# A linear-attention and gated-MLP kernel: the first batch loaded in two halves of heads through casting DMAs, and block 0's output phase moved behind its own gate and value products

## The chip, the cores and the metric

The kernel runs on one core of one Trainium2 chip. The metric is the device time of one execution in microseconds (us). Differences under about 0.5% are not told apart from no change.

## The reference

```
kv  = einsum('bhsd,bhse->bhde', k, v)            # q, k, v: (8, 8, 576, 64) fp32
o   = einsum('bhsd,bhde->bhse', q, kv)
x   = o / sqrt(mean(o*o, -1) + 1e-6) * g_norm    # then (4608, 512): 4608 tokens, 512 = 8 heads x 64
hid = gelu(x @ w_gate) * (x @ w_val)             # (512, 1536) each
out = x + sigmoid(x @ w_res) * (hid @ w_out)     # (512, 512) and (1536, 512)
```

## The kernel before

Each batch b has 576 tokens. The first 512 of them make block b: four groups j of 128 tokens. The last 64 tokens of two neighbouring batches make one group of the ninth block (blk = 8). Everything is cast to fp16 and multiplied on TensorE (PE) into PSUM.

**Attention of a batch.** `by_token_q` and `by_token_k` (L101, L107) regroup q and k from "by head" to "by token" with a copy; `a_qT` transposes q on PE; `a_kv` (L150) sums k^T v over tokens, six pieces of 96 rows per pair of heads, and a VectorE (DVE) multiply with `mask` keeps the two diagonal 64x64 blocks; `a_o` multiplies q by it, with a square on ScalarE (ACT) and a sum on DVE; `a_norm` (L209) makes 1/rms with twelve small DVE operations; `a_t` scales; `a_xT` (L254) transposes x for the MLP; `a_x` multiplies x by g for the residual. In odd batches `a_rem_qT` and `a_rem_o` do the same for the 64 remaining tokens of two batches.

**MLP of a block.** `m_gval` (L291) makes one slice f of 128 hidden features: 4 matmuls of 512 columns with w_gate, 4 with w_val, a gelu on ACT and a product on DVE into `hid`. There are 12 slices. `m_out(blk, j)` (L312) makes the output of 128 tokens: 4 matmuls with w_res, 12 with w_out, then tanh, two DVE operations and a store.

**Order.** Each engine runs its instructions in the order in which the program issues them. The loop at L431 goes over nine blocks. A block has 12 slots of `m_gval`, then four of `m_out` of the block before it; the last block has four more for its own. `attn_plan(blk + 1)` (L407) spreads the next batch's attention over the slots, one list of steps per slot. In block 0 there is no block before, so there are 12 slots only, and the plan starts in slot 7: its later steps stand behind the last slot, with no MLP work between them. The loads of later batches are issued from GpSimd's queue (POOL), which casts fp32 to fp16 on the way; `load_batch` needs the `kr` and `qraw` buffers free.

**Start.** Batch 0 is loaded in fp32 from SyncE's queue (SP), q, then k and v in halves of heads (L346 to L350), cast and regrouped by ACT, DVE and POOL (L381 to L391), multiplied, normalised in four groups of 512 columns (`a_norm_by_sqrt`, L230) and then transposed group by group inside `m_gval_first` (L300), which runs slices f = 0 and 1 for one group of tokens (a chunk) at a time. The weights' loads are issued behind the cast of v on POOL (L388).

Of the kernel before, what the change touches and what calls it, by code (L numbers as in the profile page):

```python
# [18 lines left out]
def kernel(  # L19
# [15 lines left out]

# [51 lines left out]
    def tiles_16(b):  # L87
        b16_t[b, "q"] = qkvp.tile([P, NJ, H, D], FP16, tag="q16", name="q16")
        b16_t[b, "k"] = qkvp.tile([KP, NI, H, D], FP16, tag="k16", name="k16")
        b16_t[b, "v"] = qkvp.tile([KP, H, NI * D], FP16, tag="v16", name="v16")  # L90

    def load_batch(b):
        tiles_16(b)
        raw[b, "k"] = stage.tile([KP, H, NI * D], FP16, tag="kr", name="kr")
        raw[b, "q"] = stage.tile([P, H, NJ * D], FP16, tag="qraw", name="qraw")
        nc.gpsimd.dma_start(out=raw[b, "k"], in_=src_kv(k, b, 0, H))  # L96
        nc.gpsimd.dma_start(out=b16_t[b, "v"], in_=src_kv(v, b, 0, H))
        nc.gpsimd.dma_start(out=raw[b, "q"], in_=src_q(b, 0, H))
        load_qr(b)

    def by_token_q(b, lo, hi, copy):  # L101
        copy(
            out=b16_t[b, "q"].rearrange("p j h d -> p h j d")[:, lo:hi, :, :],
            in_=raw[b, "q"].rearrange("p h (j d) -> p h j d", j=NJ)[:, lo:hi, :, :],
        )

    def by_token_k(b, lo, hi, copy):  # L107
        copy(  # L108
            out=b16_t[b, "k"].rearrange("p i h d -> p h i d")[:, lo:hi, :, :],
            in_=raw[b, "k"].rearrange("p h (i d) -> p h i d", i=NI)[:, lo:hi, :, :],  # L110
        )
# [38 lines left out]
    def a_kv(b, lo, hi):  # L150
# [125 lines left out]
    def w_of(ws, f):  # L276
        i, o = (f * P) // WC, (f * P) % WC
# [110 lines left out]
    for i in range(4):  # L388
        load_wgv(i)
# [100 lines left out]
```

## Time and profile before

| | |
|---|---|
| time, median of 3 runs | 405.15 us (404.41 to 406.44) |
| the profiled execution: its time / its span | 404.58 us / 402.8 us |
| busy: PE / DVE / ACT / POOL | 362.3 / 216.4 / 154.6 / 36.6 us |
| moved by DMA | 30.89 MB |

The profile is of one execution; its span is counted from the first to the last instruction. A busy PE is not a PE at its peak: matmuls overlap, so the time from start to start is the measure of one. The page's slices are 40 equal parts of the span, 10.07 us each. DMA bytes count what is written, so a casting load counts its fp16 size.

### The profile page before, as it was taken

To read this page: it belongs to the slowest core of one execution; us is meant where nothing else is said; L and a number is where in the kernel's file an instruction comes from. 1 tells how busy PE (TensorE), PEld (TensorE's weight loads), DVE (VectorE), ACT (ScalarE), POOL (GpSimd) and SP (SyncE) were. 2 spreads that over 40 slices of the span, in tenths; PEclk is the share of its full clock that TensorE was granted. 3 is DMA by queue.
4 is the path that set the end of the run, shared out by engine and by line. 5 is a ranking of instruction groups with operands and counts; after the bars stand their busy time and mean duration, and the time that the engine had idled before them with its cause. 6 is when DMAs were issued, how large, how long until landed. Compare 5 with 4: busy or idle time off the path is not lost.

```text
span 402.8 us, 5424 instructions
## 1 busy us (share of the span) xinstructions
PE 362.3 (90%) x2129; PEld 185.9 (46%) x2129; DVE 216.4 (54%) x411; ACT 154.6 (38%) x252; POOL 36.6 (9%) x50
## 2 busy tenths in 40 slices
PE   2337993999999999999999999999999999999994
PEld 1327452454446444544554445445544444444441
DVE  1360457648555856585558555855585443433442
ACT  5052344555236533542364335423643232232110
POOL 0763030020011001100110011000000000000000
PEclk9999998899999999999999999999999999999999
DMA  8999978091119011901190119011001100200113
GB/s 227 176 186 197 205 114 118 2 164 13 52 52 175 3 54 52 174 3 54 54 177 1 54 53 176 1 54 52 2 0 54 52 0 28 78 0 2 73 59 78
DMA packets 38988, 30.89 MB, mean 77 GB/s; under 512 B 5682, under 2 KB 34354, under 8 KB 38962
## 3 DMA queue, kind: packets, MB, share of 16 engines
q0 software_dynamic: 30896, 17.70, 32.1%
q1 hardware_dynamic: 8066, 12.85, 9.8%
q8 instruction: 16, 0.26, 0.3%
q14 instruction: 10, 0.08, 0.1%
HBM read 38.80 MB, written 9.44 MB: 120 GB/s over the span
## 4 chain that ended last, share of the span: by engine, by line
PE 87%; DMA 5%; DVE 3%; POOL 2%; ACT 2%; issue 1%; SPq 0%; DVEq 0%; ACTq 0%
PE gps L283 24%; PE vps L283 24%; PE fps L322 23%; PE rps L317 8%; DMA vf<-in_v_dram 3%; PE kvp L158 2%; DMA qr<-in_q_dram 2%; PE xtp L259 2%; PE qtp L147 2%; PE op L179 1%; DVE t L247 1%; ACT xT L260 1%; POOL wg L122 1%; POOL wv L123 1%; DVE ss L173 1%
## 5 line engine op out<-in xcount | busy, mean ns | idle before, releaser
L274 DVE TENSOR_TENSOR hid<-ge,vps 128x512 f16<-128x512 f16 x108 | 74.0, 686 | 93.0 <-PE vps L283 80.1
L283 PE MATMUL gps<-xT,wg 128*128 128x512 f16 (+1 forms) x456 | 115.3, 378 | 3.3 <-ACT xT L260 2.5
L283 PE MATMUL vps<-xT,wv 128*128 128x512 f16 (+1 forms) x456 | 114.7, 376 | 0.0
L273 ACT ACTIVATE ge<-gps 128x512 f16<-128x512 f32 x108 | 64.6, 598 | 98.6 <-PE gps L283 91.8
L322 PE MATMUL fps<-wo,hid 128*128 128x512 f16 x432 | 99.1, 379 | 0.0
L283 PEld LDWEIGHTS <-wv 128*128 128x128 f16 x456 | 45.4, 102 | 50.9 <-issue 1.4
L322 PEld LDWEIGHTS <-hid 128*128 128x128 f16 x432 | 42.2, 98 | 51.0
L283 PEld LDWEIGHTS <-wg 128*128 128x128 f16 x456 | 43.6, 102 | 44.0 <-issue 5.7
L327 DVE SCALAR_TENSOR_TENSOR pf<-th,fps 128x512 f32<-128x512 f32 x36 | 24.7, 687 | 64.9 <-PE fps L322 64.9
L325 ACT ACTIVATE th<-rps 128x512 f32<-128x512 f32 x36 | 21.5, 597 | 57.9 <-PE rps L317 57.9
L260 ACT ACTIVATE xT<-xtp,gcol 128x512 f16<-128x512 f16 x36 | 23.2, 686 | 42.2 <-PE xtp L259 42.2
L317 PE MATMUL rps<-wr,xT 128*128 128x512 f16 x144 | 37.0, 379 | 0.0
L172 ACT ACTIVATE sq<-op 128x512 f32<-128x512 f32 x32 | 19.0, 597 | 22.6 <-PE op L179 22.0
L173 DVE TENSOR_REDUCE ss<-sq 128x8 f32<-128x512 f32 x36 | 24.4, 685 | 4.7 <-ACT sq L172 2.2
L329 DVE SCALAR_TENSOR_TENSOR osb<-pf,t 128x512 f32<-128x512 f32 x36 | 24.9, 692 | 1.2
L259 PE MATMUL xtp<-ident,t 128*128 128x128 f16 x144 | 15.1, 243 | 10.0 <-DVE t L247 10.0
L96 POOL DMA_DIRECT2D kr<-in_k_dram x7 | 5.5, 789 | 187.4 <-DVE k L108 187.4
L158 PE MATMUL kvp<-v,k 96*128 96x128 f16 x192 | 14.6, 230 | 7.1 <-POOL v L386 5.4
L148 ACT COPY qT<-qtp 128x1024 f16<-128x1024 f16 x16 | 16.1, 1012 | 10.5 <-PE qtp L147 10.5
L317 PEld LDWEIGHTS <-xT 128*128 128x128 f16 x144 | 13.4, 98 | 13.5
L259 PEld LDWEIGHTS <-t 128*128 128x128 f16 x144 | 10.3, 107 | 17.7 <-DVE t L247 15.1
L247 DVE TENSOR_TENSOR t<-op,ny 128x512 f16<-128x512 f32 x28 | 17.9, 684 | 0.3
(57 smaller groups left out, 166.3 us busy)
## 6 DMA issues: line engine op xcount, KB each, us to landing
out_dram<-osb SPq DMA_DIRECT2D x32, 256.0 KB, 2.3
kr<-in_k_dram POOLq DMA_DIRECT2D x7, 576.0 KB, 6.2
v<-in_v_dram POOLq DMA_DIRECT2D x7, 576.0 KB, 9.1
qraw<-in_q_dram POOLq DMA_DIRECT2D x7, 512.0 KB, 10.9
wg<-in_moe_w_gate_dram POOLq DMA_DIRECT2D x6, 256.0 KB, 7.5
wv<-in_moe_w_val_dram POOLq DMA_DIRECT2D x6, 256.0 KB, 8.5
wo<-in_moe_w_out_dram POOLq DMA_DIRECT2D x1, 1536.0 KB, 18.6
kf<-in_k_dram SPq DMA_DIRECT2D x2, 576.0 KB, 10.4
```

The costliest lines, as they stand in the source:

```text
L158: nc.tensor.matmul(ps[:, pr, :], lhsT=k16[:, i, pr * P : (pr + 1) * P], rhs=v16[:, 2 * pr : 2 * pr + 2, i * D : (i + 1) * D], start=(i == ...
L173: nc.vector.tensor_reduce(out=st[b]["ss"][:, j, :], in_=sq, op=ALU.add, axis=mybir.AxisListType.X)
L247: nc.vector.tensor_tensor(out=t_t[blk][:, jj, :].rearrange("p (h d) -> p h d", h=H), in0=s["o"][j].rearrange("p (h d) -> p h d", h=H), in1 ...
L259: nc.tensor.transpose(ps[:, cc, :], t_t[blk][:, jj, cc * P : (cc + 1) * P], ident)
L260: nc.scalar.activation(out=xT_t[blk][:, :, jj * P : (jj + 1) * P], in_=ps, func=AF.Copy, scale=gcol)
L273: nc.scalar.activation(out=ge, in_=gps, func=AF.Gelu)
L274: nc.vector.tensor_tensor(out=hids[blk][:, f, :], in0=ge, in1=vps, op=ALU.mult)
L283: nc.tensor.matmul(ps[:, j0 * P : j1 * P], lhsT=w[:, cc, :], rhs=xT_t[blk][:, cc, j0 * P : j1 * P], start=(cc == 0), stop=(cc == NP - 1),)
L317: nc.tensor.matmul(rps, lhsT=xT_t[blk][:, cc, js], rhs=wr16[:, cc, :], start=(cc == 0), stop=(cc == NP - 1))
L322: nc.tensor.matmul(fps, lhsT=hid[:, f, js], rhs=wo16[:, f, :], start=(f == 0), stop=(f == NF - 1))
L327: nc.vector.scalar_tensor_tensor(out=pf, in0=th, scalar=1.0, in1=fps, op0=ALU.add, op1=ALU.mult)
L329: nc.vector.scalar_tensor_tensor(out=osb, in0=pf, scalar=0.5, in1=t_t[blk][:, j, :], op0=ALU.mult, op1=ALU.add)
```

## The change

Batch 0 is loaded by six casting DMAs on POOL's queue (q, k, v of heads 0 to 3, then of heads 4 to 7). The tokens keep the layout "by head", and each head is used from there: no cast, no regrouping. The last 64 tokens' k and v come in fp32 through SP, 16 rows of four tokens, and are cast by DVE. PE gets 22 matmuls on zeros (`keep_warm`) in between. Attention of batch 0 runs per half of heads; the norm and the transposes go by half and by group (`first_norm`, `first_xT`), partly inside the chunks of `m_gval_first`.

For the other batches, k and v are split like q: four pieces of 128 rows and one of 64 (`kl`, `vl`, two more DMAs per batch), so `a_kv` has 5 matmuls per pair of heads for 6. The gate and value weights come as slices of 256, 256, 512 and 512 columns, all ahead of batch 1; w_out comes in three pieces.

Every block is followed by its own output phase. For block 0 that phase goes by slices of w_out (`out_by_f`): four slots with w_res, then 12 slots of 4 matmuls, one for each group of tokens, with batch 1's attention between them; its stores stand in block 1. The plan of later blocks starts in slot 0.

The core of the diff:

```diff
-            for i in range(NI):
+            cs = slice(pr * P, (pr + 1) * P)
+            for j in range(NJ):
                 nc.tensor.matmul(
                     ps[:, pr, :],
...
+            nc.tensor.matmul(ps[:, pr, :], lhsT=kl[:, cs], rhs=vl[:, cs], start=False, stop=True)
...
+    def out_by_f(blk):
+
+        ths, fpss, pfs = [], [], []
+        slots = [lambda j=j: ths.append(m_res(blk, j)) for j in range(NJ)]
+
+        def step(f):
+            if f == 0:
+                fpss.extend(pmoe.tile([P, C], FP32, tag="mm", name="fps") for _ in range(NJ))
+            for j in range(NJ):
+                m_ffn(blk, j, f, fpss[j])
+            if f == NF - 1:
+                pfs.extend(m_gate(ths[j], fpss[j]) for j in range(NJ))
+
+        slots += [lambda f=f: step(f) for f in range(NF)]
+        return slots, [lambda j=j: m_store(blk, j, pfs[j]) for j in range(NJ)]
...
+    kl32, vl32 = as_rows("kl32"), as_rows("vl32")
+    for t32, t in ((kl32, k), (vl32, v)):
+        nc.sync.dma_start(out=t32, in_=t[0, :, M0:S, :].rearrange("h (p j) d -> p h (j d)", j=NJ))
...
+    load_first("q", q, 0)
+    load_first("k", k, 0)
     ident32 = consts.tile([P, P], FP32, name="ident32")
     make_identity(nc, ident32)
+    load_first("v", v, 0)
+    for n, t in (("q", q), ("k", k), ("v", v)):
+        load_first(n, t, 1)
...
+    nc.vector.tensor_copy(out=kl16, in_=kl32)
+    nc.vector.tensor_copy(out=vl16, in_=vl32)
...
+    def keep_warm(n):
+        for _ in range(n):
+            nc.tensor.matmul(idle, lhsT=zeros[:, 0:P], rhs=zeros, start=True, stop=True)
...
+    def first_kv(half):
+        ps = pattn.tile([P, 2, D], FP32, tag="at", name="kvp")
+        for e2 in range(2):
+            for e in range(2):
+                h = 4 * half + 2 * e2 + e
+                for i in range(2 * NJ):
+                    js = slice((i % NJ) * D, (i % NJ + 1) * D)
+                    kk, vv = (kl16, vl16) if i < NJ else (first["k"], first["v"])
+                    nc.tensor.matmul(
+                        ps[e * D : (e + 1) * D, e2, :],
+                        lhsT=kk[:, h, js],
+                        rhs=vv[:, h, js],
...
+    def first_norm(half, j0, n):
...
+        nc.scalar.activation(out=sq, in_=ps.rearrange("p j (h d) -> p j h d", h=HH), func=AF.Square)
+        nc.vector.tensor_reduce(out=s0["ss"][:, js, hs], in_=sq, op=ALU.add, axis=mybir.AxisListType.X)
+        nc.scalar.activation(
+            out=rms0[:, js, hs], in_=s0["ss"][:, js, hs], func=AF.Sqrt, bias=eps_col, scale=1.0 / D
+        )
+        nc.vector.reciprocal(out=rinv0[:, js, hs], in_=rms0[:, js, hs])
+        for j in range(n):
+            nc.vector.tensor_tensor(
...
+    keep_warm(9)
+    first_qT(0)
+    keep_warm(3)
+    first_kv(0)
+    first_qT(1)
+    first_o(0, 0, 2, pmoe, "mm")
+    first_o(0, 2, 2, pmoe, "mm")
+    first_norm(0, 0, 2)
+    keep_warm(4)
+    first_kv(1)
+    first_norm(0, 2, 2)
+    keep_warm(2)
+    for j in range(NJ):
+        first_o(1, j, 1, pattn, "at")
+    first_norm(1, 0, 1)
+    keep_warm(2)
+    first_xT(0, 0, 2, False)
+    first_norm(1, 1, 1)
+    keep_warm(2)
+    first_xT(1, 0, 1, False)
+    for i in range(len(WCS)):
         load_wgv(i)
...
+        if j == 0:
+            first_xT(0, 2, 2, True)
+            first_norm(1, 2, 1)
+            first_xT(1, 1, 1, False)
+        elif j == 1:
+            first_norm(1, 3, 1)
+            first_xT(1, 2, 1, False)
+            nc.scalar.preload_act_table_set("gelu_and_others")
+        elif j == 2:
+            first_xT(1, 3, 1, True)
...
+            slots = [lambda: m_gval_first(0, first_chunk), None]
             slots += [lambda f=f: m_gval(0, f) for f in range(2, NF)]
-            plan.setdefault(4, []).extend(lambda j=j: a_x(0, j) for j in range(NJ))
+            outs, stores = out_by_f(0)
+            slots += outs
+            plan[2] = [g_rows]
+            plan[4] = [lambda j=j: a_x(0, j) for j in range(NJ)]
         else:
             slots = [lambda f=f: m_gval(blk, f) for f in range(NF)]
-            slots += [lambda j=j: m_out(blk - 1, j) for j in range(NJ)]
-        if blk == B:
             slots += [lambda j=j: m_out(blk, j) for j in range(NJ)]
```

Three places show the new order of instructions.

The first DMAs of POOL's queue (128x4x256 is one half of four heads, fp16; wg and wv are the gate and value weights). Before:

```order
masks.py:199 AFFINE_SELECT ident_122<-ident_122 128x128
L386 CAST v_107<-vf 96x1536
L122 DMA wg_91<-in_moe_w_gate_dram 128x4x256
L123 DMA wv_92<-in_moe_w_val_dram 128x4x256
L122 DMA wg_93<-in_moe_w_gate_dram 128x4x256
```

Now:

```order
L386 DMA q_110<-in_q_dram 128x4x256
L386 DMA k_111<-in_k_dram 128x4x256
masks.py:197 MEMSET ident_115 128x128
masks.py:199 ISA
masks.py:199 AFFINE_SELECT ident_115<-ident_115 128x128
L386 DMA v_112<-in_v_dram 128x4x256
L386 DMA q_110<-in_q_dram 128x4x256
L386 DMA k_111<-in_k_dram 128x4x256
L386 DMA v_112<-in_v_dram 128x4x256
L112 DMA wg_91<-in_moe_w_gate_dram 128x4x256
L113 DMA wv_92<-in_moe_w_val_dram 128x4x256
```

Batch 0 now heads this queue, and the first weights stand behind its six pieces, with no cast ahead of them.

DVE's queue at the first slices of block 0 (hid is the product of gelu and value; grow and g are the row of g_norm and its copy on all partitions, which a matmul of PE makes between the two). Before:

```order
L401 CAST grow_138<-grow 1x512
L404 CAST g_137<-gbp 128x512
L274 TENSOR_TENSOR hid<-ge,vps 128x512 x5
L266 TENSOR_TENSOR t<-t,g_137 128x512 x4
L274 TENSOR_TENSOR hid<-ge,vps 128x512 x3
```

Now:

```order
L263 TENSOR_TENSOR hid<-ge,vps 128x512 x3
L557 CAST grow_143<-grow 1x512
L560 CAST g_142<-gbp 128x512
L263 TENSOR_TENSOR hid<-ge,vps 128x512 x2
L255 TENSOR_TENSOR t<-t,g_142 128x512 x4
L263 TENSOR_TENSOR hid<-ge,vps 128x512 x7
```

The cast that PE's one g_norm matmul waits for has moved behind the third slice's product; that matmul stands on PE between slices 2 and 3.

ACT's queue at the end of block 0 (ge is the gelu, th the tanh of the output phase, qT and xT the copies behind transposes, sq the squares). Before:

```order
L172 ACTIVATE sq<-op 128x512
L205 COPY o_588<-orp 128x512
L172 ACTIVATE sq<-orp 128x512
L172 ACTIVATE sq<-op 128x512 x3
L260 ACTIVATE xT<-xtp,gcol 128x4x128 x5
L273 ACTIVATE ge<-gps 128x512 x3
```

Now:

```order
L262 ACTIVATE ge<-gps 128x512 x12
L315 ACTIVATE th<-rps 128x512 x2
L143 COPY qT<-qtp 128x1024
L315 ACTIVATE th<-rps 128x512
L143 COPY qT<-qtp 128x1024
L315 ACTIVATE th<-rps 128x512
L189 COPY qtr_138<-qtrp 128x4x64
L190 COPY qtr_140<-qtrp 128x4x64
L171 ACTIVATE sq<-op 128x512
```

Batch 1's attention no longer starts among the gelus of block 0; it starts among the four tanhs of block 0's output phase.

## Rows read from the trace of the kernel before

**Rows 1.** The page's slices: each digit or figure is one fortieth of the span.

```profile
PE   2337993999999999999999999999999999999994
...
PEclk9999998899999999999999999999999999999999
...
GB/s 227 176 186 197 205 114 118 2 164 13 52 52 175 3 54 52 174 3 54 54 177 1 54 53 176 1 54 52 2 0 54 52 0 28 78 0 2 73 59 78
```

**Rows 2.** The page's chain that ended last: shares of the span by engine.

```profile
PE 87%; DMA 5%; DVE 3%; POOL 2%; ACT 2%; issue 1%; SPq 0%; DVEq 0%; ACTq 0%
```

**Rows 3.** Timeline, first 17 us: start, us, engine, line, operation [idle before <-releaser].

```profile
4.55 1.04 ACT L102 CAST q<-qf 128x1024 f16<-128x1024 f32 x1 [2.53 <-DMA qf<-in_q_dram]
...
12.84 1.46 POOL L386 CAST v<-vf 96x1536 f16<-96x1536 f32 x1 [11.53 <-DMA vf<-in_v_dram]
...
16.39 0.96 DVE L391 CAST v<-vf 96x1536 f16<-96x1536 f32 x1 [0.44 <-DMA vf<-in_v_dram]
```

**Rows 4.** Timeline, PE in block 0: the first four, and two later, groups of full-width matmuls.

```profile
40.35 1.91 PE L283 MATMUL gps<-xT,wg 128*128 128x512 f16 x4
...
42.05 1.79 PE L283 MATMUL vps<-xT,wv 128*128 128x512 f16 x4
...
46.27 1.03 PE L283 MATMUL vps<-xT,wv 128*128 128x512 f16 x4
...
47.14 1.03 PE L283 MATMUL gps<-xT,wg 128*128 128x512 f16 x4
```

**Rows 5.** Timeline, PE from the end of block 0 into block 1.

```profile
69.86 3.00 PE L259 MATMUL xtp<-ident,t 128*128 128x128 f16 x20 [5.74 <-DVE t L247]
...
73.04 1.64 PE L283 MATMUL gps<-xT,wg 128*128 128x512 f16 x4 [0.17 <-ACT xT L260]
...
75.38 1.03 PE L283 MATMUL gps<-xT,wg 128*128 128x512 f16 x4
```

**Rows 6.** Stretches: us, busy us (instructions) of PE, PEld, DVE, ACT, POOL, PEclk, DMA share, GB/s.

```profile
17.00:21.00 4.00, 2.81 (x26) 2.65 (x26) 1.16 (x3) 0.75 (x2) 4.00 (x6) 1.00 1.29 165
...
20.00:24.00 4.00, 1.49 (x14) 1.22 (x12) 2.88 (x6) 3.21 (x9) 3.60 (x5) 1.00 1.35 173
...
70.00:72.00 2.00, 2.00 (x16) 1.23 (x14) 2.00 (x4) 1.49 (x3) 0.00 (x0) 0.50 0.00 0
```

**Rows 7.** The tile wg: its six loads, from issue to landing.

```profile
DMA to landing us min/median/max: 4.2/7.5/13.4
```

**Rows 8.** Timeline, POOL's DMA issues at 15 to 18 us.

```profile
15.13 1.13 POOL L123 DMA_DIRECT2D wv<-in_moe_w_val_dram  x1
...
16.25 1.41 POOL L122 DMA_DIRECT2D wg<-in_moe_w_gate_dram  x1
...
17.64 0.75 POOL L123 DMA_DIRECT2D wv<-in_moe_w_val_dram  x1
```

**Rows 9.** Groups of instructions by shape: count | busy us, mean ns of one | idle before.

```profile
L173 DVE TENSOR_REDUCE ss<-sq 128x8 f32<-128x512 f32 x36 | 24.4, 685 | 4.7 <-ACT sq L172 2.2
L260 ACT ACTIVATE xT<-xtp,gcol 128x512 f16<-128x512 f16 x36 | 23.2, 686 | 42.2 <-PE xtp L259 42.2
...
L172 ACT ACTIVATE sq<-op 128x512 f32<-128x512 f32 x32 | 19.0, 597 | 22.6 <-PE op L179 22.0 <-DVE ss L173 0.5
...
L235 ACT ACTIVATE rms<-ss,eps_col 128x8 f32<-128x8 f32 x4 | 1.0, 292 | 0.2 <-DVE ss L173 0.2
...
L238 DVE RECIPROCAL rin<-rms 128x8 f32<-128x8 f32 x4 | 0.8, 193 | 0.0
```

**Rows 10.** Timeline, PE: twelve k^T v matmuls and what follows them.

```profile
56.66 0.84 PE L158 MATMUL kvp<-v,k 96*128 96x128 f16 x12
...
57.34 1.03 PE L283 MATMUL gps<-xT,wg 128*128 128x512 f16 x4
```

**Rows 11.** The chain in order of time, output phase: start, us, what.

```profile
373.74 2.59 PE fps L322 x12
377.19 2.59 PE fps L322 x12
```

More of the change, by code (lines that the diff above doesn't have):

```diff
@@ L101, in by_token_q @@
[L101 to L110, printed above, removed]
+        b16_t[b, "k"] = qkvp.tile([P, NJ, H, D], FP16, tag="k16", name="k16")
@@ L380, with first_qT @@
     attn_begin(0)
[L381 to L388 removed]
+    s0 = st[0]
+    s0["kv2"] = kv2_0
+    xT0, t0 = xT_t[0], t_t[0]
+    rms0 = consts.tile([P, NJ, H], FP32, name="rms0")
+    rinv0 = consts.tile([P, NJ, H], FP32, name="rinv0")
+    def first_qT(half):
+        for e2, copy in enumerate((nc.scalar.copy, nc.vector.tensor_copy)):
+            pr = 2 * half + e2
+            ps = pattn.tile([P, NJ, P], FP16, tag="at", name="qtp")
+            for j in range(NJ):
+                for e in range(2):
+                    nc.tensor.transpose(
+                        ps[e * D : (e + 1) * D, j, :], first["q"][:, 2 * pr + e, j * D : (j + 1) * D], ident
+                    )
+            copy(out=s0["qT"][:, :, pr, :], in_=ps)
@@ new lines, with first_o @@
+    op0 = {}
+    def first_o(half, j0, n, pool, tag):
+        ps = pool.tile([P, n, HH * D], FP32, tag=tag, name="op")
+        op0[half, j0] = ps
+        for j in range(n):
+            for e2 in range(2):
+                pr = 2 * half + e2
+                nc.tensor.matmul(
+                    ps[:, j, e2 * P : (e2 + 1) * P],
+                    lhsT=s0["qT"][:, j0 + j, pr, :],
+                    rhs=kv2_0[:, pr, :],
+                    start=True,
+                    stop=True,
+                )
@@ new lines, in first_xT @@
+    def first_xT(half, j0, n, on_vector):
+        ps = pattn.tile([P, 2, n, P], FP16, tag="at", name="xtp")
+        for j in range(n):
+            for e2 in range(2):
+                cc = 2 * half + e2
+                nc.tensor.transpose(ps[:, e2, j, :], t0[:, j0 + j, cc * P : (cc + 1) * P], ident)
+        dst = xT0[:, 2 * half : 2 * half + 2, j0 * P : (j0 + n) * P].rearrange("p c (j t) -> p c j t", j=n)
+        if on_vector:
+            nc.vector.tensor_scalar(out=dst, in0=ps, scalar1=gcol, scalar2=None, op0=ALU.mult)
+        else:
+            nc.scalar.activation(out=dst, in_=ps, func=AF.Copy, scale=gcol)
@@ L453 @@
                 load_batch(1)
-                load_wgv(4)
-                load_wgv(5)
                 nc.gpsimd.dma_start(out=wr16, in_=moe_w_res.rearrange("(cc p) c -> p cc c", p=P))
-                nc.gpsimd.dma_start(out=wo16, in_=moe_w_out.rearrange("(ff p) c -> p ff c", p=P))
-            if s == (12 if blk == 0 else 3) and blk + 2 < B:
-                load_batch(blk + 2)
+                for f in range(0, NF, 4):
+                    load_wo(f, f + 4)
+        assert not plan
+        if blk == 0:
+            late = stores
 _INS = ['q', 'k', 'v', 'g_norm', 'moe_w_gate', 'moe_w_val', 'moe_w_out', 'moe_w_res']
```

213 lines of the change are left out of this document (121 added, 92 removed).

## The prediction

> **What bounds the kernel now.** First the slices of the span [rows 1]: PE reads 9 tenths in every slice but six. The losses lie ahead: the first four slices, 40 us, read 2, 3, 3 and 7, and the seventh, from 60 us, reads 3; the last holds the final stores. The chain that ended last [rows 2] says the same: 87% PE, and what is left is DMA, DVE, ACT and POOL at the front. So later blocks can only gain by fewer matmuls, and the front by ending sooner.
>
> The front: q's first half lands at 4.55 us and the two halves of v at 12.84 and 16.39, each cast before use [rows 3]. After that comes a serial chain of norm, transposes and chunks, and the first full-width matmuls start at 40.35 us [rows 4]. Those run four in 1.70 us (42.05 − 40.35), 0.43 us per 512 columns, the 1.2 GHz level, although the slices print a granted clock of 9 there; at 46 to 47 us four take 0.87 us, 0.216 each, the 2.4 GHz level [rows 4]. I go by the spacing.
>
> The hole: behind block 0's last slot PE waits 5.74 us for batch 1's norm, transposes from 69.86 us and starts block 1 at 73.04; that slice takes 2.34 us (75.38 − 73.04) instead of 1.73 [rows 5], at the granted clock 0.50 that the stretch just before has [rows 6].
>
> **The sum**, on the profiled execution (span 402.8 us, time 404.58, 0.57 below the median of 405.15).
>
> *Batch 0's loads.* Six casting DMAs of 0.262 MB head POOL's queue at about 0.5 us. Before, the same size and shape on an idle POOL queue, the first wg, took 4.2 us to land; six of these had a median of 7.5, behind each other [rows 7]. Then the queue moved 165 and 173 GB/s [rows 6], so 1.6 us per piece: q at 4.7, the last v at 4.7 + 5 x 1.6 = 12.7. DVE casts the 64 remaining tokens at the same time. Before, two POOL issues that met DVE's fp32 casts took 1.13 and 1.41 us where the next took 0.75 [rows 8]: 0.4 to 0.65 lost per cast. POOL issues faster than the data move, so I add 0.6 for the two: 13.3 us. The Trainium skill (SBUF — State Buffer, "SBUF: two separate sides") says that such a cast locks GpSimd out, so that it cannot write descriptors until the cast ends. By it the two casts, together some 2.5 us if sized from the 0.96 us cast, would cost 2.5 rather than 0.6, and the sum below would be 1.9 higher. The trace agrees that there is a loss, at half that size.
>
> *From there to full-width matmuls.* Operations are half the width of before; between 512 columns (0.6 on ACT, 0.69 on DVE) and 8 columns (0.29 and 0.19) [rows 9] I take 0.4. k^T v: 32 matmuls of 64 columns, not in the trace; between half of a 128-column one and one at the low level, 0.03 to 0.11, I take 0.06, since 128 columns take 0.68/12 = 0.057 at the high level [rows 10]: 1.9, and 0.6 with drain and copy, 15.8. ACT and DVE first finish the norm of heads 0 to 3 (square 0.60, sum 0.69, root 0.29): 17.4. Then for a quarter of the rest: reciprocal and two products of the earlier part 1.1, sum 0.4, root 0.3, reciprocal 0.2, product 0.4: 19.8. In ACT's order the next quarter's square, sum and root (1.1) stand ahead of the transposed copy, its product ahead of the first chunk: about 22.1. A quarter costs square, sum, root, reciprocal, product and copy in turn, 0.4 + 0.4 + 0.3 + 0.2 + 0.4 + 0.45 = 2.15, so chunks start at 22.1, 24.2 and 25.9; the third and fourth are PE's own, 16 x 0.057 = 0.9 each. Full width starts at **27.7**, where it was 40.35.
>
> *Block 0's slices.* Ten of 8 x 0.216 = 1.73: 17.3. The g_norm matmul stands behind slice 2 on PE and waits for a cast behind three products on DVE. Those begin some 0.9 us after the chunks, take 0.69 each [rows 9], 2.95, and the cast (0.19 to 0.69, taken 0.4) makes 3.35, when PE has been free since 1.73: with the matmul **1.9** lost, and queued behind it is slice 3 and everything else on PE.
>
> *Output phase of block 0 with batch 1's attention.* 64 matmuls: the last blocks show 3.45 us per group of tokens (377.19 − 373.74) [rows 11], 13.8 in all. 84 small ones x 0.057 = 4.8. DVE's path: kv2 ends about 6.4 us after the phase starts, five squares and sums reach to 12.1, twelve small operations of 0.19 and a gap make 14.8, the first product 15.4. PE is at that transpose at 14.8: 0.7 wait, 0.4 at the next. All four PSUM buffers hold w_out sums to the end, and block 1's first slice waits for DVE's first gating (0.69) behind the last: 1.0. **20.7** together.
>
> *The rest.* From 73.04 to the end are 329.8. Off: 0.6 for the slow slice, as PE no longer idles before it; 13.8 for block 0's output, now ahead; 24 matmuls (4 of 24 in batches 2 to 7) x 0.057 = 1.4. **314.0**. The four late stores' DVE operations hide under block 1's matmuls; were DVE behind, each would cost 0.69. DMAs kl and vl add two issues of 0.75 per batch on POOL, 38 us ahead of use, nothing. In later blocks `m_out` reads its own last slice, 0.96 us of gelu and product after PE is done; 15 matmuls (3.2 us) cover it.
>
> 27.7 + 17.3 + 1.9 + 20.7 + 314.0 = 381.6 of span; the time lies 1.8 above the span: **383.4 us**, 21 less (5.2%).
>
> *Weights.* Ahead of w_res's end stand 7.3 MB. At 176 to 197 GB/s (slices three and four, [rows 1]) and 2 us of start that is 39 to 43 us, plus 2 for uneven engines, against a need at 46.9. Free by 2 us or more; w_out's first third (2.8 us later) is needed 5.7 us later.
>
> **Rivals.**
>
> *The front's loads come later.* The first piece lands at 6 us and each next takes 2.2 (0.262 MB at 120 GB/s), since SP's 0.26 MB and DVE's casts fall into the same start. The last v lands at 17.0 and the serial chain shifts whole, +3.7: **387**. For: the casting queue's first stretches, 165 and 173, lie below the later 186 and 197. Against: before, the same start on an idle queue gave 1.6 per piece while POOL met two casts as well.
>
> *The clock is low at the start of block 0.* The 22 zero matmuls are 22 x 512 columns, and PE waits for data between them. If 512 columns stay at 0.43, the chunks last 1.7 instead of 0.9, which puts full width at 31.2, and its first two groups lose 0.83 each as they did before [rows 4]: 3.5 + 1.7, **388.6**. The Trainium skill (TensorE: Matmul & The Clock Gate, "HAM oscillation — how this bites in real kernels") says that bursts with DMA waits between them fall back to half rate each time. Here the level stayed at 1.2 GHz through all of the interrupted chunks up to 40 us, which agrees with it. For the high level speaks that PE now starts with nine full-width matmuls in a row and has more of them in the waits; before, it had none until 40 us.
>
> *Weights late.* If DMA runs at 160 GB/s, w_res lands at 50: PE stands 3 us ahead of the output phase: **386.5**.
>
> *Slower.* `m_out` directly behind its own slices turns into a wait in every block. The spare is 3.2 − 0.96 = 2.3 us, so it decides from a DVE backlog above that; a backlog of 5.2 us is a wait of 2.9 in each of eight blocks, 23 us: **406**. Against it: DVE holds 3% of the chain that ended last [rows 2], and most of that lies in the front.
>
> *The hole stays.* The change fills the hole only if the norm is done in time. If batch 1's chain on DVE ends 3 us later than I lay it out, most of the 5.74 us [rows 5] come back, 5.1 instead of 2.1: **386.4**.
>
> **How the numbers follow.** Forecast 0.57; late loads 0.13; low clock 0.14; late weights 0.05; hole 0.07; slower 0.02; 0.02 for a larger gain. The lower bounds of the unknown costs together (loads at 1.3 us per piece, 1.5 less; k^T v at 0.03, 1.0 less; no wait for g_norm, 1.9 less; half the waits of the output phase, 1.0 less) give 378; the upper end takes in each single rival but the slower one and half of a second beside the low clock: 391. About 0.5%, 2 us, is what a measurement can tell from no change. Faster by more 0.97; within 0.01; slower 0.02.
>
> **What would show it.** The last of the six loads at about 13 us, the first full-width matmul at 27 to 28 with groups of four 0.87 apart, a PE wait of 1 to 2 us behind slice 2, no idle above 1 us between there and block 1's start near 68, blocks 39 us apart. Wrong it is if full width starts after 32, if its first groups are 1.7 apart, or if waits of over 1 us stand at the head of each later output phase.

## The result, and the profile after

The changed kernel takes 386.8 us (median of 4 runs, 386.1 to 388.2) beside 405.0 us of the kernel before in the same session (404.4 to 406.4): a ratio of 0.955, 95% interval 0.951 to 0.959. The gain is 18.2 us; 383.4 us were forecast, within a range of 378 to 391. The profiled execution took 386.48 us with a span of 384.7.

The page's slices of the changed kernel, each one fortieth of the span (rows named as in [rows 1]):

```profile
PE   5968999999999999999999999999999999999993
...
PEclk9769999999999999999999999999999999999999
...
GB/s 115 197 205 192 204 82 123 30 199 66 31 80 169 17 29 79 139 50 28 56 146 68 0 83 99 114 0 83 29 2 0 55 57 0 8 75 28 0 38 73
```

The page's chain that ended last, shares of the span by engine:

```profile
PE 91%; DVE 4%; DMA 2%; ACT 1%; issue 1%; POOL 0%; DVEq 0%; POOLq 0%
```

Against [rows 1], the weak seventh slice is gone, and the first four slices read 5, 9, 6 and 8 instead of 2, 3, 3 and 7; zero matmuls are part of these digits, so they flatter the front. Against [rows 2], PE rose from 87 to 91% of the chain. The first DMA rate fell from 227 to 115 GB/s: this is the start in which the six casting loads run. The two figures can't be compared as they stand, since the loads before wrote fp32 and these write fp16, half the bytes for the same tokens.

The front of the changed kernel in the timeline (start, us, engine, line, operation, idle time before and what ended it), the loads and the first heads:

```profile
1.19 4.00 PE L429 MATMUL idle<-zeros 128*128 128x512 f16 x9 [1.19 <-DVE zeros L397]
...
6.71 0.64 PE L446 MATMUL qtp<-ident,q 128*64 128x128 f16 x16 [1.52 <-DMA q<-in_q_dram]
...
7.03 1.34 POOL L112 DMA_DIRECT2D wg<-in_moe_w_gate_dram  x1
...
10.38 0.38 PE L459 MATMUL kvp<-v,k 128*64 128x64 f16 x4 [1.99 <-DMA v<-in_v_dram]
...
14.46 1.43 PE L429 MATMUL idle<-zeros 128*128 128x512 f16 x4
14.63 0.74 POOL L113 DMA_DIRECT2D wv<-in_moe_w_val_dram  x1 [0.54 <-DMA v<-in_v_dram]
15.82 0.31 PE L459 MATMUL kvp<-vl,kl 16*64 16x64 f16 x4
...
22.13 0.61 PE L511 MATMUL xtp<-ident,t 128*128 128x128 f16 x4 [2.61 <-DVE t L499]
```

The reader is to see three times: q's first half is used at 6.71 us (4.55 in [rows 3], but there a cast still followed), the first v at 10.38, the last v is in at 14.6 (the POOL row, an issue that waits for it). The second half's k^T v starts only at 15.82, 1.2 us after its data, behind four zero matmuls. Nine zero matmuls in 4.00 us follow each other at about 0.43, the 1.2 GHz level of [rows 4].

Then PE into block 0, and from block 0's output phase into block 1:

```profile
25.53 0.63 PE L274 MATMUL gps<-xT,wg 128*128 128x128 f16 x4
25.95 0.63 PE L274 MATMUL vps<-xT,wv 128*128 128x128 f16 x4
...
31.22 1.02 PE L274 MATMUL gps<-xT,wg 128*128 128x512 f16 x4
32.08 1.03 PE L274 MATMUL vps<-xT,wv 128*128 128x512 f16 x4
34.27 0.37 PE L559 MATMUL gbp<-grow,ones 1*128 1x512 f16 x1 [1.17 <-DVE grow L557]
34.58 1.04 PE L274 MATMUL gps<-xT,wg 128*128 128x512 f16 x4
...
66.35 0.40 PE L248 MATMUL xtp<-ident,t 128*128 128x128 f16 x4 [0.43 <-DVE t L236]
66.95 0.40 PE L248 MATMUL xtp<-ident,t 128*128 128x128 f16 x4 [0.20 <-DVE t L236]
...
69.58 1.03 PE L319 MATMUL fps<-wo,hid 128*128 128x512 f16 x4
70.75 1.04 PE L274 MATMUL gps<-xT,wg 128*128 128x512 f16 x4
71.62 1.03 PE L274 MATMUL vps<-xT,wv 128*128 128x512 f16 x4
...
95.81 1.02 PE L306 MATMUL rps<-wr,xT 128*128 128x512 f16 x4
```

Full-width matmuls start at 31.22 where they started at 40.35 [rows 4], and at the 2.4 GHz level at once (0.86 apart; 1.70 in [rows 4]). The first chunk still ran at the lower one: 0.42 from group to group of small matmuls at 25.5 us. Before block 1 the 5.74 us of [rows 5] have become 0.43 and 0.20, and the slow first slice of block 1 is gone.

So the 18 us come from three stretches. Up to full width 9.1 us are gained (40.35 to 31.22). From there to block 1 the change takes 39.53 us, 13.8 of them for block 0's output phase, and the kernel before took 32.69 without it: 7.0 gained. From block 1 to the end it takes 384.7 − 70.75 = 313.95 us instead of 329.8, of which 13.8 are the output phase that is already done: 2.0 gained.

Two rows of the kernel before split the 9.1 us (its second half's k^T v, and its first chunk):

```profile
17.40 1.44 PE L158 MATMUL kvp<-v,k 96*128 96x128 f16 x12 [1.62 <-DVE v L391]
...
29.49 0.59 PE L283 MATMUL gps<-xT,wg 128*128 128x128 f16 x4 [0.78 <-DMA qr<-in_q_dram]
```

The second k^T v starts 1.6 us sooner (15.82), from it to the first chunk it takes 9.7 us instead of 12.1, and from there to full width 5.7 instead of 10.9. So the earlier data give the smallest part; the norm and the chunks behind them give the rest. That is read from two traces: no run puts the old loads or the old norm back by itself.

### The profile page after: what moved, and what is told of

Its sections match the earlier page's. It is cut to its first block, busy times and chain, and to the rows that moved or that the text cites. A ratio compares the mean times of both kernels' runs of the same rounds, so it can differ in the third digit from the quotient of the medians.

```text
span 384.7 us, 5547 instructions
## 1 busy us (share of the span) xinstructions
PE 368.1 (96%) x2179; PEld 185.5 (48%) x2179; DVE 217.2 (56%) x425; ACT 151.2 (39%) x256; POOL 49.0 (13%) x67
## 4 chain that ended last, share of the span: by engine, by line
PE 91%; DVE 4%; DMA 2%; ACT 1%; issue 1%; POOL 0%; DVEq 0%; POOLq 0%
PE gps L274 24%; PE vps L274 24%; PE fps L319 22%; PE rps L306 8%; PE kvp L156 2%; DMA v<-in_v_dram 2%; PE xtp L248 2%; PE qtp L142 2%; PE op L178 2%; PE kvp L163 1%; PE kvp L459 1%; DVE pf L325 1%; DVE t L236 1%; PE xtp L511 0%; PE orp L196 0%
## 5 line engine op out<-in xcount | busy, mean ns | idle before, releaser
L274 PE MATMUL gps<-xT,wg 128*128 128x512 f16 (+1 forms) x456 | 113.0, 371 | 0.2
L274 PE MATMUL vps<-xT,wv 128*128 128x512 f16 (+1 forms) x456 | 112.7, 370 | 0.0
L249 ACT ACTIVATE xT<-xtp,gcol 128x512 f16<-128x512 f16 x32 | 20.5, 684 | 37.6 <-PE xtp L248 37.6
L88 POOL DMA_DIRECT2D qraw<-in_q_dram x7 | 6.2, 888 | 173.5 <-DVE q L97 136.6
L172 DVE TENSOR_REDUCE ss<-sq 128x8 f32<-128x512 f32 x32 | 21.9, 686 | 5.6 <-ACT sq L171 3.3
L171 ACT ACTIVATE sq<-op 128x512 f32<-128x512 f32 x28 | 16.7, 597 | 12.7 <-PE op L178 12.7
L306 PEld LDWEIGHTS <-xT 128*128 128x128 f16 x144 | 13.3, 98 | 13.8 <-issue 1.4
L143 ACT COPY qT<-qtp 128x1024 f16<-128x1024 f16 x14 | 14.2, 1013 | 8.8 <-PE qtp L142 8.8
L255 DVE TENSOR_TENSOR t<-t,g 128x512 f16<-128x512 f16 x36 | 13.6, 418 | 0.0
L178 PEld LDWEIGHTS <-qT 128*128 128x128 f16 x112 | 8.6, 98 | 6.6
L248 PEld LDWEIGHTS <-t 128*128 128x128 f16 x128 | 8.6, 98 | 5.3 <-DVE t L236 1.3
## 6 DMA issues: line engine op xcount, KB each, us to landing
wo<-in_moe_w_out_dram POOLq DMA_DIRECT2D x3, 512.0 KB, 13.8
```

Source lines behind the costliest of these rows:

```text
L171: nc.scalar.activation(out=sq, in_=ps, func=AF.Square)
L172: nc.vector.tensor_reduce(out=st[b]["ss"][:, j, :], in_=sq, op=ALU.add, axis=mybir.AxisListType.X)
L249: nc.scalar.activation(out=xT_t[blk][:, :, jj * P : (jj + 1) * P], in_=ps, func=AF.Copy, scale=gcol)
L274: nc.tensor.matmul(ps[:, j0 * P : j1 * P], lhsT=w[:, cc, :], rhs=xT_t[blk][:, cc, j0 * P : j1 * P], start=(cc == 0), stop=(cc == NP - 1),)
L306: nc.tensor.matmul(rps, lhsT=xT_t[blk][:, cc, j * P : (j + 1) * P], rhs=wr16[:, cc, :], start=(cc == 0), stop=(cc == NP - 1),)
```

## The experiments

Ten kernels ran beside the change. The table has their times: the ratio is to the kernel before, in the same session; the two starts are those of the profiled execution, and small differences between them are partly differences between executions.

| kernel | median us | ratio, 95% interval | full width starts | block 1 starts |
|---|---|---|---|---|
| the change | 386.8 | 0.955 (0.951 to 0.959) | 31.22 | 70.75 |
| e1 no zero matmuls | 386.97 | 0.956 (0.954 to 0.959) | 31.90 | 71.43 |
| e2 more zero matmuls | 385.51 | 0.952 (0.950 to 0.955) | 30.38 | 69.91 |
| e3 g_norm's cast early | 386.27 | 0.954 (0.951 to 0.957) | 33.34 | 71.64 |
| e4 casts on ACT | 387.08 | 0.958 (0.955 to 0.960) | 31.62 | 71.19 |
| e5 rest by POOL's DMAs | 387.52 | 0.958 (0.956 to 0.959) | 32.30 | 71.84 |
| e6 output phase late | 395.96 | 0.979 (0.977 to 0.980) | 31.90 | 65.46 |
| e7 g_norm's loads late | 386.07 | 0.953 (0.951 to 0.955) | 31.57 | 71.10 |
| e8 zeros placed anew, cast early | 383.15 | 0.947 (0.946 to 0.949) | 29.01 | 67.32 |
| e9 e8 and e7 | 383.56 | 0.948 (0.946 to 0.951) | 29.55 | 67.86 |
| e10 e9, fewer zeros | 383.5 | 0.949 (0.945 to 0.953) | 28.73 | 67.04 |

**e1 and e2: what the zero matmuls and the clock are worth.**

```diff
# e1
-        for _ in range(n):
+        for _ in range(0):
# e2
     first_qT(0)
-    keep_warm(3)
+    keep_warm(12)
...
-    keep_warm(2)
+    keep_warm(12)
     first_xT(0, 0, 2, False)
...
-    keep_warm(2)
+    keep_warm(6)
     first_xT(1, 0, 1, False)
```

> The 22 matmuls on zeros are left out. Theory A (the fills pay): without them TensorE stays at the 1.2 GHz level through batch 0, so each chunk of 16 matmuls takes 1.7 us and the first full-width slices still come four in 1.7 us; full width starts at 32 to 33 us instead of 31.2 and 1.7 to 3 us more are lost behind it: 388.5 to 391 us. Theory B (the fills cost what they stand for): in the changed kernel two chunks ran at the low level in any case and four fills took 1.23 us between the two k^T v sums, on the chain; without them that time comes back: 385 to 386.5 us.

> More fills where the changed kernel's TensorE waited: 12 instead of 3 ahead of the first k^T v, 12 instead of 2 ahead of the first transposes of x, 6 instead of 2 ahead of the next. Theory A (the low level in 8 to 15 and 22 to 29 us comes from the waits just before): the granted clock stays at 1.00 from 7 us on, the first k^T v takes 1.9 instead of 2.3 us, chunks 0.9 instead of 1.7; full width starts at 28 to 29.5 instead of 31.2 us: 384 to 385.5 us. Theory B (the front is bound by the norm's chain on ScalarE and VectorE and by the loads, the clock is hidden): the level rises but full width moves by less than 0.5 us: 386.3 to 387.

Without zeros the kernel takes 386.97, the same within 0.2 us. The timeline of e1, second k^T v and chunks:

```profile
14.68 0.42 PE L459 MATMUL kvp<-vl,kl 16*64 16x64 f16 x4
15.03 0.42 PE L459 MATMUL kvp<-v,k 128*64 128x64 f16 x4
...
30.13 0.63 PE L274 MATMUL gps<-xT,wg 128*128 128x128 f16 x4
```

PE is at the second k^T v 1.14 us sooner (14.68, about when the last v is in), but its groups of four take 0.35 instead of 0.24 and the chunks stay at the lower level until 30.6 us. Both effects are real and nearly cancel: the 22 zeros as placed are worth 0.7 us of front in these executions and nothing that the medians show.

With more zeros the level is high from 11 us on, and the time falls to 385.51, 1.3 us below the change with intervals that overlap; in the traces the front is 0.84 us shorter, between what the two theories gave. The chunks of e2:

```profile
26.87 0.29 PE L511 MATMUL xtp<-ident,t 128*128 128x128 f16 x2 [0.72 <-DVE t L499]
...
28.29 0.29 PE L511 MATMUL xtp<-ident,t 128*128 128x128 f16 x2 [0.24 <-DVE t L499]
```

The chunks are twice as fast and now wait for the norm (0.72 and 0.24): from chunk 0 to full width 5.29 us instead of 5.69. So the low level in the chunks was nearly hidden by the norm; that is why its price is 0.4 there and not the 3.5 of the rival. And the twelve zeros ahead of the first k^T v ran partly at the low level, to 11.6 us, past the landing of the first v (10.3 to 10.6 us in the other executions with the same loads).

**e3: g_norm's cast inside the chunks.**

```diff
         elif j == 2:
             first_xT(1, 3, 1, True)
+            nc.vector.tensor_copy(out=grow16, in_=grow[:, None, :].to_broadcast([1, H, D]))
...
     def g_rows():
-        nc.vector.tensor_copy(out=grow16, in_=grow[:, None, :].to_broadcast([1, H, D]))
```

> The cast of g_norm's row on VectorE is issued in the third chunk, ahead of the first products, and nothing else changes. Theory: TensorE's wait behind slice 2 (1.63 us between the end of slice 2 and the start of slice 3 in the changed kernel, with the 0.3 us matmul in it) falls to 0.2 to 0.4 us, and nothing later takes it up: 1.2 to 1.6 us less, 385.2 to 385.6 us. Rival: w_res or w_out then are late, and the wait moves to the output phase of block 0: 386.3 to 387 us.

The timeline of e3 behind slice 2:

```profile
34.20 1.03 PE L274 MATMUL vps<-xT,wv 128*128 128x512 f16 x4
35.16 0.39 PE L559 MATMUL gbp<-grow,ones 1*128 1x512 f16 x1
```

The wait is gone: from full width to block 1 it takes 38.30 us instead of 39.53, 1.23 less. The median shows 0.5 of it, and the intervals overlap. In this execution, the slowest of its four (387.37), the front itself was 2.1 us later at the low level (full width at 33.34); what the others' fronts did is not on record. The wait is shown in the trace; its price in the time is not shown by itself, only in e8 together with other edits.

**e4 and e5: who delays batch 0's loads.** In e4 ACT casts the last 64 tokens' k and v instead of DVE. In e5 they come by two casting DMAs of POOL, without SP and without a cast.

```diff
# e4
-    nc.vector.tensor_copy(out=kl16, in_=kl32)
-    nc.vector.tensor_copy(out=vl16, in_=vl32)
+    nc.scalar.copy(out=kl16, in_=kl32)
+    nc.scalar.copy(out=vl16, in_=vl32)
# e5
-        nc.sync.dma_start(out=t32, in_=t[0, :, M0:S, :].rearrange("h (p j) d -> p h (j d)", j=NJ))
...
     load_first("v", v, 0)
+    for t16, t in ((kl16, k), (vl16, v)):
+        nc.gpsimd.dma_start(out=t16, in_=t[0, :, M0:S, :].rearrange("h (p j) d -> p h (j d)", j=NJ))
```

> The two fp32 to fp16 casts of the 64 remaining tokens go to ScalarE instead of VectorE. Theory A (VectorE's casts hold up GpSimd's DMA issues): the two issues that took 1.38 and 1.34 us at 5.7 and 7.0 us take 0.75 each, bytes in 5 to 8 us go from some 120 to 180 GB/s or more, the first half of v lands at 9 to 9.5 instead of 10.3 us and full width starts 0.7 to 1.3 us earlier: 385.3 to 386 us. Theory B (the two fp32 loads into 16 partitions and the small g_norm loads slow the DMA engines themselves): issues get shorter but bytes in 3 to 8 us and the landing of v stay within 0.3 us: 386.5 to 387.

> The 64 remaining tokens of batch 0 come by two casting DMAs of 0.066 MB each on GpSimd's queue, behind the first three; SyncE's two fp32 loads into 16 partitions and the two VectorE casts are gone, and k^T v takes these tokens last. Theory A (the fp32 loads slow the DMA engines in the first 5 us): bytes in 2 to 8 us rise from 100 to 150 towards 190 GB/s, the first v lands at 9 to 9.5 instead of 10.3 us, full width starts 0.7 to 1.3 us earlier: 385 to 386 us. Theory B (this queue starts slowly whatever stands beside it): the first v lands at 10 to 10.5 us as before, and 386 to 387.5 us.

POOL's issues and the landing of v in e4:

```profile
5.64 0.78 POOL L386 DMA_DIRECT2D v<-in_v_dram  x1
...
6.38 0.79 POOL L112 DMA_DIRECT2D wg<-in_moe_w_gate_dram  x1
...
10.33 0.37 PE L459 MATMUL kvp<-v,k 128*64 128x64 f16 x4 [2.07 <-DMA v<-in_v_dram]
...
14.60 0.74 POOL L113 DMA_DIRECT2D wv<-in_moe_w_val_dram  x1 [0.57 <-DMA v<-in_v_dram]
```

The two issues take 0.78 and 0.79 instead of 1.38 and 1.34, so DVE's casts do hold POOL up by 0.6 each, as [rows 8] had it. But v lands where it landed: the first half at 10.33 against 10.38, the last at 14.60 against 14.63. The loss is not on the path. In e5 the first v came about 1 us sooner (9.34), as theory A had it, but the k and v of the last tokens later (10.48) and the last v at 14.6 as before. Neither gains in time: 387.08 and 387.52 lie just above what theory B gave for each.

**e7: the three loads of g_norm behind the six.**

```diff
-    nc.sync.dma_start(out=gcol[0:D, :], in_=g_norm.unsqueeze(1))
-    nc.sync.dma_start(out=gcol[D : 2 * D, :], in_=g_norm.unsqueeze(1))
...
-    nc.sync.dma_start(out=grow, in_=g_norm.unsqueeze(0))
...
         load_first(n, t, 1)
+    nc.gpsimd.dma_start(out=gcol[0:D, :], in_=g_norm.unsqueeze(1))
+    nc.gpsimd.dma_start(out=gcol[D : 2 * D, :], in_=g_norm.unsqueeze(1))
+    nc.gpsimd.dma_start(out=grow, in_=g_norm.unsqueeze(0))
```

> The three loads of g_norm (64 rows of 4 bytes twice, one row) are issued on GpSimd's queue behind the six loads of batch 0 instead of on SyncE's at 1.6 to 2.9 us. Theory A (these small writes hold the DMA engines up): bytes in 4 to 8 us rise from some 110 to 170 GB/s or more and the first v lands at 9.3 to 9.8 instead of 10.3 us, full width 0.5 to 1 us earlier: 385.5 to 386.3 us. Theory B: no change before 8 us, and three more issues ahead of the weights that nothing waits for: 386.3 to 387.3.

Stretches (us, busy us and instructions of PE, PEld, DVE, ACT, POOL, then granted clock, DMA share, GB/s) of the changed kernel:

```profile
5.00:8.00 3.00, 1.48 (x20) 0.69 (x19) 3.00 (x5) 0.59 (x1) 3.00 (x3) 1.00 1.05 121
8.00:10.00 2.00, 0.38 (x5) 0.37 (x5) 0.38 (x2) 0.00 (x0) 2.00 (x4) 0.61 1.39 185
10.00:14.00 4.00, 3.62 (x48) 3.07 (x48) 0.55 (x2) 0.84 (x2) 2.73 (x4) 0.50 1.45 196
```

The first of them in e7, PE's row with the first v, and POOL's row that shows the last v:

```profile
5.00:8.00 3.00, 2.26 (x20) 1.10 (x19) 3.00 (x5) 0.58 (x1) 3.00 (x3) 1.00 1.40 182
```

```profile
8.83 0.37 PE L459 MATMUL kvp<-v,k 128*64 128x64 f16 x4
...
13.87 0.74 POOL L112 DMA_DIRECT2D wg<-in_moe_w_gate_dram  x1 [0.61 <-DMA v<-in_v_dram]
```

With three loads of 256 bytes each, two of them in rows of 4 bytes, at the start the DMA engines moved 121 GB/s from 5 to 8 us; without them there it is 182. The other traces agree: with them e1 to e4, e6 and e8 have 95 to 111 GB/s in this stretch, without them e9 and e10 have 185 and 180. q is used at 5.96 instead of 6.71, the first v at 8.83 instead of 10.38, and the last v is in at 13.9 instead of 14.6 (without the small loads 13.5 to 14.5 in e7, e9 and e10; with them 14.5 to 14.8 in all others). The time did not follow (386.07, intervals overlap): in this execution, the slowest of its four (387.19), the four zeros and the second k^T v ran at the low level, and k^T v with the last v began at 15.11. What the earlier loads are worth in the time is not shown.

**e6: the output phases where they were.** The edit moves those of all blocks back, and the place at which batch 1's attention starts. Its core:

```diff
-            outs, stores = out_by_f(0)
-            slots += outs
...
-            slots += [lambda j=j: m_out(blk, j) for j in range(NJ)]
+            slots += [lambda j=j: m_out(blk - 1, j) for j in range(NJ)]
+            if blk == B:
+                slots += [lambda j=j: m_out(blk, j) for j in range(NJ)]
```

> Block 0 has no output phase of its own: every block's output follows the next block's slices, batch 1's attention starts in slot 7 of block 0 as in the kernel before; all else is as in the changed kernel. Theory: the hole behind block 0's last slot comes back, a wait of 5 to 6 us for the norm and the low clock at the head of block 1; block 1 starts at 63 to 65 us with 13.8 us of output still to do, where the changed kernel has none left at 70.8: 6.5 to 8 us more, 393.3 to 395 us. Rival (the waits inside the output phase by slices are as long as the hole): under 3 us more, below 390.

```profile
62.28 3.00 PE L248 MATMUL xtp<-ident,t 128*128 128x128 f16 x20 [5.68 <-DVE t L236]
65.46 1.86 PE L274 MATMUL gps<-xT,wg 128*128 128x512 f16 x4 [0.18 <-ACT xT L249]
68.22 1.03 PE L274 MATMUL gps<-xT,wg 128*128 128x512 f16 x4
```

The hole is back with 5.68 us, where 5.74 stood in [rows 5], and block 1's first slice is slow again (2.76 us to 68.22). It costs 9.2 us, half of the whole gain and more than the 6.5 to 8 that were expected. By the rows: 5.68, another wait of 0.77 ahead of it, 1.9 for 20 transposes at the low level (3.0 instead of 20 x 0.057), 1.0 of the slow slice, 0.7 that the front of this execution lay later, less the waits of 1.3 in the change's own output phase: 8.8, against 9.0 between the spans. The later blocks have no part in it: from block 1 to the end e6 takes 328.2 us, and the change's 313.95 with 13.8 for the output phase and 1.0 for the slow slice are 328.8.

**e8 to e10: what the front can still give.** e8 places the zeros as 9, 8, 1, 2, 12, 6 and casts g_norm early as e3 does. e9 adds the edit of e7, and e10 takes five zeros instead of eight there.

```diff
# e8, beside e3's edit
     first_qT(0)
-    keep_warm(3)
+    keep_warm(8)
...
-    keep_warm(4)
+    keep_warm(1)
     first_kv(1)
...
-    keep_warm(2)
+    keep_warm(12)
     first_xT(0, 0, 2, False)
...
-    keep_warm(2)
+    keep_warm(6)
     first_xT(1, 0, 1, False)
# e10, beside e9
-    keep_warm(8)
+    keep_warm(5)
```

> Fills of 9, 8, 1, 2, 12 and 6 instead of 9, 3, 4, 2, 2 and 2, and the early cast of g_norm's row. The two gains are in different places (full width at 30.4 instead of 31.2 us; 1.23 us of wait behind slice 2) and should add; without the four fills ahead of the second k^T v another 0.5 to 1 us, if the level stays high. Theory: full width at 29.5 to 30.2 us, block 1 at 67.8 to 68.5, 383.2 to 384.5 us. Rival (the level drops between, or chunks wait for the norm's chain all the same): full width no earlier than 30.4, 384.5 to 385.3.

> The three changes that helped by themselves, together: the zero matmuls placed as in the run with fills and g early (9, 8, 1, 2, 12, 6), the cast of g_norm inside the chunks, and the three small loads of g_norm behind the six casting loads. Theory A (the small loads delay the casting loads, the low level delays the rest, and the two add up): q lands at 6.0 instead of 6.7, the last v at 13.9 instead of 14.6, the second half's k^T v starts at 13.9 to 14.1 instead of 14.3, full width at 28.4 to 28.7 instead of 29.0, time 382.4 to 382.9 against 383.15 for the run without the moved loads. Rival (PE's own work ahead of the second k^T v, eight zero matmuls that run to 10.9 us, decides and not the loads): k^T v starts at 14.2 to 14.4, full width at 29.0, time 383.0 to 383.4, no difference.

> As the run with all three, with five zero matmuls instead of eight ahead of the first k^T v. At 0.43 us each eight of them end near 10.2 to 10.9 us, while the first v lands near 8.7; five end near 9. Theory A (the fills' length decides there): the first k^T v starts at 9.0 instead of 10.2 or later, and the front gains up to 1 us where the second v (13.9) does not hold it: full width at 28.0 to 28.4, time 382.0 to 382.6. Rival (the second half's v, the norm chain and the level decide): the second k^T v still waits for v at 13.9 and full width comes at 28.4 to 29; or the level is low when k^T v starts because fewer zeros precede it (0.35 per four small matmuls instead of 0.24), which costs 16 x 0.11 = 1.8 on the first k^T v: time 383 to 384.5.

The timeline of e8:

```profile
14.31 0.31 PE L459 MATMUL kvp<-vl,kl 16*64 16x64 f16 x4
...
23.72 0.39 PE L274 MATMUL gps<-xT,wg 128*128 128x128 f16 x4
...
30.83 0.39 PE L559 MATMUL gbp<-grow,ones 1*128 1x512 f16 x1
```

e8 is the best of all, 383.15 us: 3.6 below the change (3.1 by the ratios), with intervals apart. Full width starts 2.2 us sooner and g_norm costs no wait. e9 and e10 don't differ from it within their intervals, so the expectation of another half microsecond failed. In e10 the loads did come sooner, and the row after them shows where it went:

```profile
13.28 0.28 PE L459 MATMUL kvp<-v,k 128*64 128x64 f16 x4 [0.58 <-DMA v<-in_v_dram]
...
16.48 4.03 PE L429 MATMUL idle<-zeros 128*128 128x512 f16 x12
20.35 0.39 PE L511 MATMUL xtp<-ident,t 128*128 128x128 f16 x4
```

The last v is used 1.3 us sooner than in e8 (14.55), but the twelve zeros took 4.03 us here and 2.75 in e8: they ran partly at the low level and held up the transposes, whose data DVE had ready at 19.3. A fill is sized in columns and paid in time, and its time depends on the level that it is to raise. Whether fewer zeros at that one place bring e10 below e8 was not tried.

## Why the prediction was right, and which term was off

The size was right: 18.2 us gained, 21 forecast, the time inside the range, and nothing on the other side. Four of the five totals in the sum stand as forecast, but two of the four, the output phase and the rest, do so because errors in their parts cancel. That is luck.

- **Full width at 27.7:** measured 31.2, **the term that failed, by 3.5 us**, and with it the whole miss of the time. Its parts, along the steps of the prediction:
  - *Batch 0's loads, 13.3:* the last v came at 14.6, 1.3 late. The first piece is all of it: it was used at 6.71 where 4.7 was forecast, and the five behind it took 7.9 us, 1.6 each as forecast. Of these 2.0 us, 0.75 is the first issue (1.25 us and not 0.5) and some 0.75 the three small loads on SP's queue (6.71 against 5.96 in e7), which the prediction did not count at all; for 0.5 no run shows the cause. The term for DVE's casts, 0.6, was not on the path (e4) and hid that much of it.
  - *Second k^T v directly behind the last v:* it started 1.2 us after it. Not the last v but the first decided: it landed at 10.38 (1.6 us per piece from 4.7 would be 7.9; 1.5 of the delay is gone in e7). Behind it PE worked 3.25 us on k^T v and q's transposes and 0.8 on the products, all at the low level, and 1.36 on four zeros, partly at it (0.34 each). That the zero matmuls cost time of their own was left out of the sum. Either the zeros or the level was enough for the 1.2: without zeros e1 is there at 14.68 at the low level, and in e2 the same work with its four zeros takes 3.82 us at the high one (11.87 to 15.69), which from 10.38 ends at 14.2.
  - *From there to chunk 0, 8.8:* 9.7 in the change, 9.4 in e8 at the high level. 0.6 is the serial chain of norm and transposes being somewhat longer than summed, 0.3 the level.
  - *Chunks, 5.6:* 5.7; the low level is nearly hidden behind the norm's pace, as e2 shows. The sum has a slip here: by its own 2.15 per quarter the third chunk starts at 26.4 and not at 25.9, and full width at 28.2. The measured step is 1.6, so the slip did no harm.
- **Slices 17.3 and g_norm 1.9:** 50.13 − 31.22 = 18.9 measured, 19.2 forecast. The wait is the row of the cast: PE is done at 32.95 and goes on at 34.58, 1.63 us, for the reason named (e3 removes it).
- **Output phase of block 0 with batch 1's attention, 20.7:** 70.75 − 50.13 = 20.6. Its three waits were forecast as 0.7, 0.4 and 1.0 and come out of the spacing of the rows as 0.58, 0.38 and 0.31, 0.8 less; its 20 matmuls of k^T v take 0.8 more than forecast, as the next item shows.
- **The rest, 314.0:** 313.95, and this is where luck was largest. The sum took 1.4 us off for 24 fewer matmuls of k^T v. The rows show that these got slower instead. Two pairs of heads took 0.68 us with twelve matmuls [rows 10]; now one pair alone takes 0.48 with five:

```profile
79.82 0.42 PEld L156 LDWEIGHTS <-k 128*128 128x128 f16 x4
80.04 0.39 PE L156 MATMUL kvp<-v,k 128*128 128x128 f16 x4
80.35 0.09 PEld L163 LDWEIGHTS <-kl 64*128 64x128 f16 x1
80.36 0.23 PE L163 MATMUL kvp<-vl,kl 64*128 64x128 f16 x1
80.52 0.40 PE L156 MATMUL kvp<-v,k 128*128 128x128 f16 x4
```

  The weight load of the 64-row piece (`kl`) starts together with its matmul, where that of the four before starts 0.22 us ahead. A batch takes 1.94 us for k^T v instead of 1.35, so the six batches cost 3.5 us more and not 1.4 less. What hid it is a wait of the kernel before, which the sum did not count. It stood ahead of the output phase in each of blocks 1 to 6, here in block 1:

```profile
96.64 1.03 PE L283 MATMUL vps<-xT,wv 128*128 128x512 f16 x4
98.14 0.40 PE L259 MATMUL xtp<-ident,t 128*128 128x128 f16 x4 [0.47 <-DVE t L247]
98.74 0.40 PE L259 MATMUL xtp<-ident,t 128*128 128x128 f16 x4 [0.20 <-DVE t L247]
```

  By the spacing it is 1.0 us. In the change these transposes stand between the groups of the output phase, and 0.1 is left ahead of it (95.81 in the rows above), so some 5.5 us are gained in six blocks. The two errors, 4.9 and 5.5, nearly cancel, and a new wait for q in block 1, 0.5 by the spacing, takes up what is left. Whether the change is faster still with its old k^T v pieces was not tried. Later blocks start 39.8 and 40.2 us apart (70.75, 110.51, 150.73) without a wait of over 0.1 us at the head of their output phases; the prediction's last part had 39.
- **Weights:** w_res landed 12.0 us after its issue at 31.0, so at 43.0, inside the 41 to 45 given, and was needed at 50.

**The rivals.** *Late loads* and *low clock* each came true in part and at a fraction of their price: 1.3 of 3.7 us, and about 2 of 5.2 (the 1.2, 0.3 and 0.4 above). That full width came at 31.2, the very figure of the low-clock rival, is a coincidence: the chunks were not what cost it. The late loads came true in the first piece (6.71, where the rival had 6) and not in the pace behind it (1.6 and not 2.2), with SP's small loads as a part of the cause (e7) and not DVE's casts (e4). The clock's price was too high because it assumed that PE bounds the chunks (the norm does) and that the first two full-width groups stay slow (they did not: 0.86 apart). Most of what it cost lay ahead, between 10 and 16 us, where no price had been set. The profile shows the fall after a stretch in which PE did little: in 8 to 10 us PE is busy 0.38 of 2.00 us and the granted clock falls to 0.61, then 0.50, and the second fall, to 0.52 at 22 us, follows the idle 2.61 us ahead of the transposes at 22.13. The rule of the Trainium skill (TensorE: Matmul & The Clock Gate, "HAM oscillation — how this bites in real kernels"), that bursts with DMA waits between them fall back to half rate each time, agrees with the first of these falls; the second wait was for DVE.

*The hole stays* did not come true, and e6 shows that the order does it: 9.2 us more without it. *Weights late* and *slower* did not come true.

The rule weighed in the prediction, the Trainium skill's (SBUF — State Buffer, "SBUF: two separate sides") on DVE shutting GpSimd out, agrees with e4's issues (0.78 instead of 1.38) in kind, but the full length of the casts was not lost: 0.6 beside casts of 1.51 and 1.40. In the time it was worth nothing here.

## What to carry to other kernels

A serial front is better summed along the chain of what PE does than along the loads alone: what stands in PE's queue between two loads, zero matmuls included, can make an early load decide and a late one not. Count every DMA that runs in the same stretch, however little it carries. Place zero matmuls where PE would idle anyway, and none directly ahead of work whose data are already there. Price matmuls by the spacing in the rows and not by their number: five took longer than six here. And where a total comes out as forecast, check its terms before trusting it.

## What the runs showed of the hardware that was not expected

- With three loads of g_norm, two of them in rows of 4 bytes, at the start the core's DMA moved 121 GB/s from 5 to 8 us, where 182 were moved without them (e7); e9 and e10 repeat it with 185 and 180.
- Five k^T v matmuls, four with 128-row weights and one with 64-row weights, take 0.48 us per pair of heads, where six with 96-row weights took 0.34. The weight load at each change of row count starts with its matmul and not ahead of it. Whether the row count alone does this no run shows.
- The same work gets another clock level in the front from execution to execution: e3's front was 2.1 us later in the profiled execution than the change's, with nothing changed ahead of 25 us, and its four zeros ahead of the second k^T v took 1.85 us instead of 1.36. The mean granted clock over the span (0.971 to 0.978 in four runs of e3, 0.981 to 0.995 in four of the change) does not rank fronts: e1, whose front has the low level's spacing, reads 0.996 to 0.998.
- The granted clock in the rows does not always tell the level: the nine zeros at the start have 1.00 beside a spacing of 0.43 us for 512 columns, and e1's stretches from 10 to 28 us print 1.00 as well, while its groups have the low level's spacing. The spacing of matmuls of one shape is the safer reading.
- Groups of four k^T v matmuls of 64 columns follow each other at 0.24 us (0.06 each) at the high level and 0.35 (0.09 each) at the low one, a factor of 1.5 and not 2; groups of four with 128 columns at 0.22 and 0.43. The first kind alternate between 16-row and 128-row weights; what 64 columns take without that is not shown.
